# Order and queues of the first loads, and the PSUM banks of the last two value products, in windowed attention followed by a mixture of experts

## The chip, the core and the metric

The kernel runs on one core of a Trainium2 chip. A core has TensorE (PE in the profile: matmuls, with weight loads shown as PEld), VectorE (DVE), ScalarE (ACT), GpSimd (POOL) and SyncE (SP), which here only issues DMAs. ScalarE and GpSimd can issue DMAs too. The metric is the device time of one execution in microseconds (us), the median of several runs.

## What is computed

Eight batches of eight heads, 576 positions, head width 64. Attention looks back over a window of 64 positions. Its result, 4608 tokens of width 512, goes to a mixture of experts: each token goes to the one expert of eight with the largest logit, passes two weight matrices with a ReLU between them, and is scaled by the softmax weight of its expert.

```
scores = q @ k.T / 8                       # batch 8, heads 8, S = 576, D = 64
mask   = (rel >= 0) & (rel < 64)           # rel = query position - key position
attn   = softmax(where(mask, scores, -1e9))
x      = (attn @ v) as (4608, 512)
logits = x @ w_gate                        # 8 experts
e      = argmax(logits);  gate = softmax(logits)[e]
y      = gate * (relu(x @ w1[e]) @ w2[e])  # w1[e]: 512 x 1024, w2[e]: 1024 x 512
```

## The kernel before

**Tiling.** Two batches (`BG` = 2) form a group, two heads a pair; a pair in a group of batches is a *unit*. There are `NU` = 16 units, four to each group. A unit has nine tiles of 128 positions, of which three make a *step*; so `N` = 48 steps, three (`NST`) to a unit.

**Stages of a step.** They are functions, and each is written for its own step number:

- `turned(s)` (L578): PE turns q and k (L595, or L587 for the last 64 positions of the sequence, the *rests*), and ScalarE copies the result to SBUF (L600, L590).
- `scored(s)` (L606): PE multiplies q and k into banks 0 and 1, one for each head (L628).
- `masked(s)` (L634): VectorE adds the mask and takes the row's extreme (L641). `softened(s)`: ScalarE takes the exponential (L651).
- `flipped(s)` (L654): PE turns the weights (L659). VectorE copies the first head's half to SBUF, ScalarE the second's (both L661).
- `weighted(s)` (L665): PE multiplies the weights with v into a tile `px` in bank 6 (L674). v carries a column of ones, so that the row's sum comes with it.
- `divided(s)` (L680): VectorE takes the reciprocal of the sum and multiplies (L684, L685, L688), which empties `px`.
- `x_turned(s)` (L693) and `logit(s)` (L704): PE turns the result (L699, copy L702) and multiplies with the gate's weights `wg` (L711, bank 7).

**Order.** Every engine works through its instructions in program order, which is written out by hand in `step(s)` (L941): scores of step s+1, values of s-1, flip of s, division of s-1, turn of s+3, and so on. In its middle, at each unit's first step, it issues the loads ahead: `load_v(u + 2)` and `load_qk(u + 3)`, and `load_rests` once for each group. Work listed in `todo` is issued at its step, among it the load of w1 of expert 0 in four parts of 512 KB, on ScalarE's queue (L933), at steps 1, 2, 4 and 5. The loop starts at step -3, so `turned(0)` to `turned(2)` and `scored(0)` come before step 0.

**Loads.** `load_qk(u)` (L537) makes eight DMAs of 128 KB: for each batch q of both heads, then k of both heads. `load_rests(bg)` (L548) makes six DMAs for a group of batches: two each of q, k and v. `load_v(u)` (L561) makes four DMAs of 128 KB, after which GpSimd makes a copy of v that is shifted by 64 positions (L567, L569, L573). All these are issued by SyncE, in the program's order. There are slots for eight loads in flight that SyncE and ScalarE share: in the built program each load waits for the landing of the one eight places before it. q and k have three buffers, v has three.

**End of attention.** After the last step, `weighted(N - 1)` runs, then `turn()` (L302) turns the first gathered tokens of expert 0 (L306, copied by ScalarE, L307), the last logits and divisions follow, and `hidden(0)` (L336) starts the first expert's tile: its products go to banks 0, 1 and 6 (`hps`, L264). From there on it is expert after expert, tile after tile.

The lines of the first loads before the change:

```
        load_qk(0)
        nc.sync.dma_start(out=wg[:, :, 0:E], in_=moe_w_gate.rearrange("(g p) e -> p g e", p=P))
        nc.sync.dma_start(out=x_dram[NT : NT + 1, :], in_=zrow[:])
        load_rests(0)
        load_v(0)
        load_qk(1)
        load_v(1)
        load_qk(2)
```

Of the kernel before, what the change touches and what calls it, by code (L numbers as in the profile page):

```python
# [36 lines left out]
def kernel(  # L37
# [10 lines left out]
    nc = tc.nc  # L48
# [74 lines left out]
    banks = [Memory(banks_p.tile([P, 512], F32, name=f"bank{i}")) for i in range(8)]  # L123
# [110 lines left out]
    VW = D + 1  # L234
    ST = 3
# [260 lines left out]
    with tc.manual_schedule(), ExitStack() as held, ExitStack() as brief:  # L496
# [32 lines left out]
        qks, rests, Ts, xss, xTs, lgs, logits_of = {}, {}, {}, {}, {}, {}, {}  # L529
# [7 lines left out]
        def load_qk(u):  # L537
            bg, g = units[u]
            qks[u] = [qk_m(((u % 3 + 2) % 3 * 2 + n) * 1024, BG, NV, 2, D) for n in range(2)]
            for i in range(BG):  # L540
                for t, src in zip(qks[u], (q, k)):
                    for h in range(2):
                        nc.sync.dma_start(
                            out=t[:, i, :, h, :],
                            in_=src[bg * BG + i, 2 * g + h, 0:SM, :].rearrange("(p j) d -> p j d", j=NV),
                        )

        def load_rests(bg):  # L548

            at = 6144 + bg % 2 * 2048  # L550
            vr = qk_m(at + 1024, BG, H, D)
            rests[bg] = [qk_m(at, H, D), qk_m(at + 512, H, D), vr]
            for t, src in zip(rests[bg], (q, k)):
                for i in range(BG):
                    nc.sync.dma_start(
                        out=t[i * D : (i + 1) * D], in_=src[bg * BG + i, :, SM:S, :].rearrange("h p d -> p h d")
                    )
            for i in range(BG):
                nc.sync.dma_start(out=vr[D:P, i], in_=v[bg * BG + i, :, SM:S, :].rearrange("h p d -> p h d"))

        def load_v(u):  # L561
            bg, g = units[u]
            va, vb = v_ring[u % NVR]
            for i in range(BG):
                for h in range(2):
                    nc.sync.dma_start(out=va[:, i, :, h, 0:D], in_=whole(v, u, i, h))
                G.tensor_copy(out=vb[D:P, i, NV - 1, :, 0:D], in_=rests[bg][2][D:P, i, 2 * g : 2 * g + 2])  # L567

                nc.gpsimd.tensor_copy(  # L569
                    out=vb[0:D, i].rearrange("p j h d -> p (j h d)"),  # L570
                    in_=va[D:P, i].rearrange("p j h d -> p (j h d)"),
                )
                nc.gpsimd.tensor_copy(  # L573
                    out=vb[D:P, i, 0 : NV - 1].rearrange("p j h d -> p (j h d)"),
                    in_=va[0:D, i, 1:NV].rearrange("p j h d -> p (j h d)"),
                )
# [25 lines left out]
        def blocks_of(t):  # L602

            return [(t // NV, t % NV * 2 + a) if t < BG * NV else (a, NB - 1) for a in range(2)]
# [60 lines left out]
        def weighted(s, pTs):  # L665
            u, c = divmod(s, NST)
            bg, g = units[u]
            va, vb = v_ring[u % NVR]
            px = banks[6](0, 2, ST, VW)
            for m in range(ST):  # L670
                for a, (bp, i) in enumerate(blocks_of(c * ST + m)):
                    vt = va[:, bp, i // 2] if i % 2 or i == 0 else vb[:, bp, i // 2 - 1]
                    for h in range(2):
                        nc.tensor.matmul(  # L674
                            px[a * D : (a + 1) * D, h, m, :], lhsT=pTs[h][:, m, a * D : (a + 1) * D],
                            rhs=vt[:, h, :], start=True, stop=True, skip_group_check=True,
                        )
            return px
# [240 lines left out]

        N = NU * NST  # L920
        load_qk(0)
        nc.sync.dma_start(out=wg[:, :, 0:E], in_=moe_w_gate.rearrange("(g p) e -> p g e", p=P))
        nc.sync.dma_start(out=x_dram[NT : NT + 1, :], in_=zrow[:])
        load_rests(0)
        load_v(0)
        load_qk(1)
        load_v(1)
        load_qk(2)

        for g in range(NG):  # L930
            step = NST * (g // 2) + g % 2 + 1
# [9 lines left out]
        def step(s):  # L941
            if 0 <= s + 1 < N:
                prs[s + 1] = softened(*masked(s + 1, scored(s + 1)))
            if 0 <= s - 1 < N:
                px = weighted(s - 1, pTs.pop(s - 1))
# [5 lines left out]
            if s >= 0 and s % NST == 0:  # L951
                u = s // NST
                if u + 3 < NU and (u + 3) % NG == 0:
                    load_rests((u + 3) // NG)
                if u + 2 < NU:
                    load_v(u + 2)
                if u + 3 < NU:
                    load_qk(u + 3)
# [25 lines left out]
        tr_ring = cycle((4, 5))  # L984
        tile0 = chain(hidden(0), turn(), output(0))
        px = weighted(N - 1, pTs.pop(N - 1))
        form_all(turn())
        logit(N - 3)
# [170 lines left out]
```

## Time and profile before

| What | us |
|---|---|
| Median of 3 runs (718.85 to 719.68) | 719.0 |
| The profiled execution | 719.24 |
| Its span, first to last instruction | 717.5 |
| PE busy | 687.2 (96%) |
| PE weight loads busy | 606.0 (84%) |
| VectorE busy | 505.1 (70%) |
| GpSimd busy | 355.2 (50%) |
| ScalarE busy | 259.9 (36%) |

The profile shows one execution. The 1.7 us between the span and its time lie around the program. In the slices of the page each digit is a share in tenths over 17.9 us; `PEclk` is the clock that TensorE was granted. In a timeline each row is a run of like instructions: start, length, engine, line of the kernel, operation, tile written and tiles read, shape and count, and in brackets how long the engine was idle before it and what ended that. A `q` behind an engine's name means its queue, here the issue of a DMA: the row's length is the issue alone, and the data land later, by the page's medians 4.0 us after the issue for q, 3.7 for k, 4.2 for v and 4.4 for a part of w1. Attention lies in the first 217 us, the experts behind it. DMA loads of q, k and v move in packets of 256 bytes: 117072 of the 137608 packets are under 512 bytes.

### The profile page before, as it was taken

The numbers are of one execution on the slowest core, as the hardware profiler recorded it, in microseconds if no ns is written. First come the engines' busy times: TensorE is split into PE (matmuls) and PEld (weight loads), VectorE is DVE, ScalarE is ACT, GpSimd is POOL, SyncE is SP. The second block draws the span as 40 slices with busy tenths as digits, with TensorE's granted clock in tenths as the row PEclk, the third lists the DMA queues.
The fourth block names the chain that finished last, engine by engine and source line by source line (L and its number), as shares of the span: only waits on it lengthen the run. The fifth ranks groups of instructions, "written<-read, shape, count | busy, mean of one in ns | idle before, by whom it ended". The sixth has DMA issues, their size and how long they took to land. (4 is left out here: it accounts for less than half of the span.)

```text
span 717.5 us, 17980 instructions
## 1 busy us (share of the span) xinstructions
PE 687.2 (96%) x6882; PEld 606.0 (84%) x6882; DVE 505.1 (70%) x1656; ACT 259.9 (36%) x655; POOL 355.2 (50%) x366
## 2 busy tenths in 40 slices
PE   4999999999879999999999999999999999999995
PEld 3787888788668898797999999899979799979995
DVE  3576898798965858685866676586667586666764
ACT  4688888788754211111211221121111121112210
POOL 4213847669376025947562257356274756263012
PEclk9899999999999999999999999999999999999999
DMA  8998889989261382716211441450171531111021
GB/s 156 219 198 182 179 167 226 223 187 244 87 193 48 124 294 67 275 61 195 104 46 61 148 144 61 123 200 34 60 274 60 189 109 46 60 38 45 16 61 57
DMA packets 137608, 94.42 MB, mean 132 GB/s; under 512 B 117072, under 2 KB 117072, under 8 KB 137490
## 3 DMA queue, kind: packets, MB, share of 16 engines
q1 hardware_dynamic: 127858, 62.16, 32.6%
q0 software_dynamic: 9056, 28.58, 12.5%
q10 hardware_dynamic: 576, 2.10, 0.9%
q8 instruction: 74, 1.21, 0.7%
q14 instruction: 44, 0.36, 0.2%
HBM read 73.94 MB, written 20.45 MB: 132 GB/s over the span
## 5 line engine op out<-in xcount | busy, mean ns | idle before, releaser
L315 DVE STREAM_TRANSPOSE v_m<-qk_m 32x256 f32<-32x256 f32 x320 | 139.3, 435 | 8.6 <-DMA qk_m<-x_dram,at_g 2.7
L275 POOL DMA_INDIRECT qk_m<-x_dram,at_g x42 | 45.4, 1081 | 176.1 <-DVE v_m L315 147.1
L344 PE MATMUL bank<-qk_m,s 128*128 128x128 f32 x1024 | 122.5, 275 | 0.6 <-DVE qk_m L365 0.6
L344 PEld LDWEIGHTS bank<-qk_m,s 128*128 128x128 f32 x1024 | 118.3, 192 | 0.8 <-issue 0.8
L651 ACT ACTIVATE pr<-pr,mx 128x128 f32<-128x128 f32 x288 | 89.7, 390 | 33.1 <-DVE mx L641 32.9
L344 PE MATMUL bank<-qk_m,w 128*128 128x128 f32 x768 | 93.8, 275 | 0.8 <-DVE v_m L384 0.8
L344 PEld LDWEIGHTS bank<-qk_m,w 128*128 128x128 f32 x768 | 90.6, 192 | 4.3 <-issue 4.0
L641 DVE CUSTOM_DVE_ANT_0 pr<-bank,mask 128x128 f32<-128x128 f32 x288 | 64.4, 286 | 28.3 <-PE bank L628 26.8
L384 DVE TENSOR_TENSOR v_m<-bank,v_m 128x256 f32<-128x256 f32 (+1 forms) x95 | 43.8, 480 | 40.8 <-PE bank L388 25.9
L295 POOL DMA_INDIRECT out_dram<-v_m,at_s x42 | 42.5, 1013 | 54.1 <-DVE v_m L384 50.4
L569 POOL COPY v_m<-v_m 64x520 f32<-64x520 f32 x32 | 19.8, 619 | 69.9 <-DMA v_m<-in_v_dram 69.1
L140 POOL TENSOR_TENSOR s<-w 128x1024 f32<-128x1024 f32 x22 | 52.2, 2375 | 0.0
L674 PEld LDWEIGHTS bank<-v_m,pT 128*64 128x64 f32 x1152 | 40.9, 140 | 12.5 <-DVE xs L688 6.7
L674 PE MATMUL bank<-v_m,pT 128*64 128x65 f32 x1152 | 47.7, 231 | 3.6 <-DVE xs L688 3.6
L351 ACT COPY qk_m<-bank 128x512 f32<-128x512 f32 x16 | 9.4, 587 | 108.6 <-PE bank L344 70.3
L388 PE MATMUL bank<-qkT_m,v_m 128*128 128x256 f32 x216 | 48.3, 379 | 0.0
L595 PE MATMUL bank<-ident,qk_m 128*128 128x128 f32 x256 | 36.8, 287 | 9.4 <-DMA qk_m<-in_q_dram 8.4
L388 PEld LDWEIGHTS bank<-qkT_m,v_m 128*128 128x128 f32 x216 | 41.0, 190 | 5.5
L327 ACT COPY qk_m<-v_m 128x512 f32<-128x512 f32 x40 | 22.7, 615 | 62.4 <-DVE v_m L315 62.4
L444 PEld LDWEIGHTS bank<-qk_m,w 128*128 128x128 f32 x320 | 43.9, 190 | 0.9 <-issue 0.7
L444 PE MATMUL bank<-qk_m,w 128*128 128x160 f32 x320 | 44.4, 299 | 0.4 <-ACT qk_m L327 0.4
L628 PE MATMUL bank<-qkT_m 64*64 64x128 f32 x1152 | 44.2, 284 | 0.1
(174 smaller groups left out, 1252.6 us busy)
## 6 DMA issues: line engine op xcount, KB each, us to landing
w<-in_moe_w_dram SPq DMA_DIRECT2D x11, 2048.0 KB, 9.7
qk_m<-in_q_dram SPq DMA_DIRECT2D x72, 128.0 KB, 4.0
qk_m<-in_k_dram SPq DMA_DIRECT2D x72, 128.0 KB, 3.7
v_m<-in_v_dram SPq DMA_DIRECT2D x64, 128.0 KB, 4.2
qk_m<-in_moe_w_dram SPq DMA_DIRECT2D x3, 2048.0 KB, 11.2
x_dram<-xs POOLq DMA_DIRECT2D x6, 512.0 KB, 4.8
x_dram<-xs POOLq DMA_DIRECT2D x3, 768.0 KB, 5.2
w<-in_moe_w_dram ACTq DMA_DIRECT2D x4, 512.0 KB, 4.4
```

Of the source, the lines that this page charges most:

```text
L140: op()
L275: G.indirect_dma_start(out=xg[c], out_offset=None, in_=x_dram[:, :], in_offset=bass.IndirectOffsetOnAxis(ap=at_g[:, c : c + 1], axis=0),)
L295: put = G.indirect_dma_start(out=out[:, :], out_offset=bass.IndirectOffsetOnAxis(ap=at_s[:, c : c + 1], axis=0), in_=ys[c], in_offset=None ...
L315: V.transpose(out=xn[b * QD : (b + 1) * QD, :, :, a * QD : (a + 1) * QD].rearrange("p c g i -> p (c g) i"), in_=rows[a * QD : (a + 1) * QD ...
L344: nc.tensor.matmul(acc[:, f, :], lhsT=a[:, g, f * P : (f + 1) * P], rhs=b[:, g, :], start=(first and f == 0 and g == 0), stop=(g == HG - 1 ...
L384: plus = lambda out, a, b: V.tensor_tensor(out=out, in0=a, in1=b, op=ALU.add)
L388: nc.tensor.matmul(acc, lhsT=a[:, f, :], rhs=b[:, f, :], start=(start and f == 0), stop=(stop and f == HF - 1), skip_group_check=True,)
L444: nc.tensor.matmul(acc[:, i], lhsT=w1[:, g, f * P : (f + 1) * P], rhs=xq[:, g].rearrange("p c s -> p (c s)")[:, 0:HALF], start=(i + g == 0 ...
L628: nc.tensor.matmul(out_, lhsT=qT[rows, t, a * WINDOW : (a + 1) * WINDOW], rhs=rhs, start=True, stop=True, skip_group_check=True,)
L641: V.tensor_tensor_reduce(out=prs[h][:, m, :], in0=scs[h][:, m, :], in1=mask[:, m0 + m, :], scale=-scale, scalar=-2 * MASKED, op0=ALU.add, ...
L651: nc.scalar.activation(out=y, in_=y, func=AF.Exp, scale=-1.0, bias=mx[:, h, m : m + 1])
L674: nc.tensor.matmul(px[a * D : (a + 1) * D, h, m, :], lhsT=pTs[h][:, m, a * D : (a + 1) * D], rhs=vt[:, h, :], start=True, stop=True, skip_ ...
```

## The change

Three things are edited. The k loads of unit 0 and of group 0's rests (six DMAs) are issued by ScalarE instead of SyncE. The order of the first loads is new: the rests and unit 1's q and k come before v, `wg` stands behind v of unit 1, and the zero row behind unit 2's q and k. And `weighted` of the last two steps, N-2 and N-1, puts its result in banks 0 and 1 instead of bank 6; `divided` reads it there.

```diff
@@ load_qk
-                for t, src in zip(qks[u], (q, k)):
+                for t, src, queue in zip(qks[u], (q, k), (nc.sync, nc.sync if u else nc.scalar)):
                     for h in range(2):
-                        nc.sync.dma_start(
+                        queue.dma_start(
@@ load_rests
-            for t, src in zip(rests[bg], (q, k)):
+            for t, src, queue in zip(rests[bg], (q, k), (nc.sync, nc.sync if bg else nc.scalar)):
                 for i in range(BG):
-                    nc.sync.dma_start(
+                    queue.dma_start(
@@ weighted
-            px = banks[6](0, 2, ST, VW)
+            px = banks[6 if s < N - 2 else s - N + 2](0, 2, ST, VW)
@@ the first loads
         load_qk(0)
+        load_rests(0)
+        load_qk(1)
+        load_v(0)
+        load_v(1)
         nc.sync.dma_start(out=wg[:, :, 0:E], in_=moe_w_gate.rearrange("(g p) e -> p g e", p=P))
+        load_qk(2)
         nc.sync.dma_start(out=x_dram[NT : NT + 1, :], in_=zrow[:])
-        load_rests(0)
-        load_v(0)
-        load_qk(1)
-        load_v(1)
-        load_qk(2)
```

On ScalarE the six DMAs stand ahead of everything else in its program, the load of its function table (1.28 us, issued with the first L600) included. In the new order of slots, unit 2's last k load is the one that waits for the landing of w1's first part, and unit 3's first q load the one that waits for its second part.

## The prediction

> **What bounds the kernel now.** I read the page first (busy time by slice), then who TensorE waited for, then the timeline of single engines where those waits lie.
>
> From the page, part 2:
>
> ```profile
> PE   4999999999879999999999999999999999999995
> ...
> PEclk9899999999999999999999999999999999999999
> DMA  8998889989261382716211441450171531111021
> ```
>
> TensorE (PE) is over 90% busy in all but four slices of 17.9 us. Three of the four can matter here: the first, where loads arrive, and slices 11 and 12 (179 to 215 us), where attention ends. Elsewhere the span is PE's own work, so an earlier start of it moves the end one for one.
>
> All waits of PE in the whole run (microseconds in total, times, longest):
>
> ```profile
> PE bank L595 <- DMA qk_m<-in_q_dram: 8.4, 4, 4.8
> PE bank L674 <- DVE xs L688: 3.6, 6, 1.2
> ...
> PE bank L587 <- DMA qk_m<-in_k_dram: 1.3, 1, 1.3
> PE bank L595 <- DMA qk_m<-in_k_dram: 0.8, 3, 0.4
> ```
>
> Line 1 is the turning of q and k (`turned`), line 2 the values' product (`weighted`) waiting until VectorE has emptied bank 6 (`divided`). These two are what the change touches. SyncE's queue at the start:
>
> ```profile
> 6.31 0.55 SPq L922 DMA_DIRECT2D wg<-in_moe_w_gate_dram  x1
> ...
> 11.46 2.53 SPq L566 DMA_DIRECT2D v_m<-in_v_dram  x4
> 14.03 1.24 SPq L543 DMA_DIRECT2D qk_m<-in_q_dram  x2
> 15.32 1.30 SPq L543 DMA_DIRECT2D qk_m<-in_k_dram  x2
> 16.67 1.30 SPq L543 DMA_DIRECT2D qk_m<-in_q_dram  x2
> 18.01 1.30 SPq L543 DMA_DIRECT2D qk_m<-in_k_dram  x2
> ```
>
> One load of 128 KB takes 0.67 us of the queue, and unit 1's q starts only at 14.03. What PE makes of it:
>
> ```profile
> 13.42 0.30 PE L587 MATMUL bank<-ident,qk_m 128*128 128x128 f32 x1 [1.28 <-DMA qk_m<-in_k_dram]
> ...
> 18.48 2.29 PE L595 MATMUL bank<-ident,qk_m 128*128 128x128 f32 x8 [2.62 <-DMA qk_m<-in_q_dram]
> 20.70 1.56 PE L628 MATMUL bank<-qkT_m 64*64 64x128 f32 x24
> 22.19 1.62 PE L674 MATMUL bank<-v_m,pT 128*64 128x65 f32 x24
> ```
>
> A wait for loads comes back once, at unit 4 (same view, later window):
>
> ```profile
> 55.99 0.63 PE L595 MATMUL bank<-ident,qk_m 128*128 128x128 f32 x4 [0.64 <-DMA qk_m<-in_q_dram]
> 57.02 0.63 PE L595 MATMUL bank<-ident,qk_m 128*128 128x128 f32 x4 [0.41 <-DMA qk_m<-in_k_dram]
> ```
>
> So between 24 and 57 us PE is full, yet the load stream is no more than just ahead of it. By stretch (the last two figures are the DMA engines' busy share and GB/s):
>
> ```profile
> 15.00:23.00 8.00, 5.27 (x51) 3.87 (x51) 1.99 (x16) 3.56 (x10) 2.83 (x6) 0.50 1.06 214
> ```
>
> With one queue issuing, the DMA engines already show a share of 1.06 at 214 GB/s, which is 0.61 us for 128 KB, close to the queue's 0.67. The end of attention, PE:
>
> ```profile
> 213.48 0.97 PE L674 MATMUL bank<-v_m,pT 128*64 128x65 f32 x24 [0.48 <-DVE xs L688]
> ...
> 216.81 0.97 PE L674 MATMUL bank<-v_m,pT 128*64 128x65 f32 x24 [0.88 <-DVE xs L688]
> 217.71 1.09 PE L306 MATMUL bank<-ident,qk_m 128*128 128x128 f32 x8
> ```
>
> **What the Trainium skill says.** "DMA: Bandwidth & Descriptors", section on issuing engines not being separate DMA queues: loads from several engines run on the same 16 DMA engines, and a second issuer saves only issue time. The 1.06 above agrees: there is little rate left to win. "Perfetto Trace Analysis", section on the HWDGE DMA instruction: an issue's reported time includes a wait for an exclusive descriptor generator. Whether ScalarE's and SyncE's issues take turns there, no row of this trace shows. "TensorE: Matmul & The Clock Gate", Part 1: the clock is halved after a window of 3.4 us with little work, in windows not tied to the kernel's start. The trace agrees: 15 to 23 us ran at 0.50. "ScalarE: Activation LUTs", section on the cost of the table load: about 1283 ns; the trace has 1.28 us.
>
> **The change part by part.** The profiled execution took 719.24 us (span 717.5), 0.24 above the median of 719.0; the sum is made against 719.24.
>
> (a) Six k loads leave SyncE's queue: 6 x 0.67 = 4.0 us less for it ahead of everything later. That is the upper end of what the stream can win if issue alone binds. If the DMA engines bind, the first 26 loads (8 of unit 0, 6 rests, 8 of unit 1, 4 of v of unit 0) take 26 x 0.61 = 15.9 us; from about 2.4 us, when the first bytes move, plus 0.6 to report, the last lands near 18.9. Before, the last of them was issued at 18.7, and a k load took 3.7 us from issue to landing (the page's median), so near 22.4: 3.5 won. I take 3.5 and keep 3.0 to 4.0.
>
> (b) wg, the zero row, v of units 0 and 1 move behind unit 1's q and k. In sum they stay in the stream ahead of unit 4, so the stream wins nothing by it, but PE's early waits change. Unit 1's q and k are issued from about 7.5 instead of 14.03, so the 2.62 us wait at 18.48 goes, and so does the 1.28 us at 13.42. What is late next: v of unit 0. It moves behind, lands near 18, and GpSimd then copies for 0.62 + 0.51 us (L569, L573), so `weighted` of step 0 runs at about 18.5 instead of 22.19. That is 3.7 earlier, plus up to 1 us if PE's clock rises sooner. v of unit 1 also lands before q and k of unit 2 now; unit 2 is needed by PE from 32 us on, less the shift, and lands by 29. wg is needed at 31.0 (L711) and lands before 21. The zero row is needed only by gathers at the end.
>
> (c) ScalarE issues six loads before its table load: 4 x 0.65 at once, then two that wait for a slot. In the program's order every load waits for the landing of the load eight places earlier, over both queues; for these two it is the landing of the first two k loads. Queued behind them are the table load and the first copies of `turned`, for which `scored` waits. ScalarE is free at about 5.8, the table load ends near 7.1 and the first copy starts there instead of 5.90. PE needs the first pair of copies only after its 16 turns, at about 5.2 + 16 x 0.27 = 9.6, and they end by 8.4: hidden, with 1.2 us to spare. If issues take turns at 1.3 us each, the first copy slips to about 9, and step 0 loses about 1 us; that is hidden under the wait for v of unit 0 in (b).
>
> (d) Loads meet w1's four loads of 512 KB, which ScalarE issues at steps 1, 2, 4 and 5. They come earlier with the steps. A SyncE load whose slot is held by one of them waits for it: before, the four v loads at 28.07 took 5.10 us instead of 2.5. Now the load that waits is unit 2's last k. Bound: from 1 us better to 1.5 worse; I take 0.
>
> From (a) to (d): PE would be 4 us or more ahead after step 1, but at unit 4 it waits for the stream again and keeps the stream's 3.5 us.
>
> (e) The banks. `weighted` of the last two steps writes banks 0 and 1, last read by `masked` of the last step, done near 210.5. So the waits of 0.48 and 0.88 us for L688 go. What is late next is ScalarE's copy of the turned weights (L661): for the first it ends at 213.15 (212.67 + 0.48), so 0.33 of 0.48 is won. For the second it ends at 216.16 (215.68 + 0.48), 0.33 earlier by the shift, so 215.83 against 216.81: 0.98 in all. After it comes `turn` (L306), which needs the gather issued at 212.85 with 3.5 us to land, 216.35; it would start at 216.73. Product x of the first tile uses bank 0 and y bank 1, both emptied by `divided` before PE gets there. Won: 0.9, bounds 0.3 and 1.0.
>
> Sum: 3.5 + 0.9 = 4.4 us. 719.24 - 4.4 = 714.8; on the median's footing 714.6.
>
> **The rivals.**
> A. The stream isn't what holds PE. With fewer collisions it stays ahead, unit 4's wait (0.64 + 0.41) goes, and PE keeps all that it wins at the start: the distance from step 2's `scored` at 25.96 to about 20.5 if its clock rises at once, 5.5. In all 5.5 + 1.05 + 0.9 = 7.45: 711.6. For it: the wait at unit 4 is only 1 us. Against it: the DMA share of 1.06.
> B. The engines are full from the first loads, two queues only interleave, and the win at the start is gone at unit 4. The banks' 0.9 and a few tenths stay: 717.9. For it: the DMA row's 8 and 9. Against it: the first slice, with wg and the zero row in it, has room.
> C. Slower: the shared slots. Unit 2's last k waits for the first w1 load, which ScalarE issues only in step 1, and SyncE's whole queue stands behind it. Before, the same kind of wait cost 2.6 us (5.10 less 2.5 at 28.07). It takes all that the stream won when it stands 2.6 + 3.5 = 6.1 us; at 8 us unit 4 is 2 us later than before: 719.24 + 2 - 0.9, 720.1 on the median's footing. For it: the queue's order fixes that wait. Against it: the w1 load takes 4.4 us from issue to landing (page), so 8 us needs a late issue as well.
>
> **How the numbers follow.** Main 0.70, A 0.13, B 0.09, C 0.08. About 0.2% (1.4 us) is what a measurement of this kernel can tell from no change. Main and A are faster: 0.83; B lies within: 0.09; C is slower: 0.08. The range runs from A's 711.6 to 717.0, where the stream wins 1.3 us only; B and C, 0.17, are left out.
>
> **What would show it.** Right: no wait of PE for q between 12 and 20 us, `weighted` of step 0 near 18.5, a wait at unit 4 of 1 us or more, and no wait for L688 in the last two steps. Wrong: no wait at unit 4 (A), `scored` of step 12 no earlier than before (B), SyncE standing over 6 us near 24 us (C).

## The result, and the profile after

| | before | after |
|---|---|---|
| Median of the comparison, 11 runs each (us) | 719.14 | 716.25 |
| Ratio | | 0.9966 [0.995, 0.9983] |
| The profiled execution (us) | 719.24 | 715.43 |
| Its span (us) | 717.5 | 713.7 |

The ratio is worth 2.4 us of 719 (1.2 to 3.6). The forecast was 4.4 us. The sign was right and the time lies in the range, but the gain was sized too large.

Part 2 of the page after, in slices of 17.8 us:

```profile
PE   6999999999889999999999999999999999999995
PEclk9999999999989999999999999999999999999999
DMA  9997889979443273616201531440271521111011
```

The first slice has filled from 4 to 6. Slice 12, at the end of attention, went from 7 to 8. The waits of PE in the whole run after (us in total, times, longest):

```profile
PE bank L595 <- DMA qk_m<-in_q_dram: 1.2, 2, 0.6
...
PE bank L674 <- POOL v_m L573: 0.8, 1, 0.8
...
PE bank L674 <- DVE xs L688: 0.7, 2, 0.5
PE bank L595 <- DMA qk_m<-in_k_dram: 0.6, 2, 0.4
```

Waiting for q fell from 8.4 to 1.2, but 4.8 of this is only a label: PE's very first wait, for the first load in before, is now put down to the mask, and it has grown to 5.8 us. Without the first wait the fall is 8.4 - 4.8 - 1.2 = 2.4 us. Waiting for L688 fell from 3.6 to 0.7. PE's timeline after, around step 0's values and at unit 4:

```profile
16.15 1.91 PE L595 MATMUL bank<-ident,qk_m 128*128 128x128 f32 x8
17.99 0.89 PE L628 MATMUL bank<-qkT_m 64*64 64x128 f32 x24
18.81 0.62 PE L674 MATMUL bank<-v_m,pT 128*64 128x65 f32 x8
20.23 0.74 PE L674 MATMUL bank<-v_m,pT 128*64 128x65 f32 x16 [0.80 <-POOL v_m L573]
20.90 0.87 PE L659 MATMUL bank<-ident,pr 128*128 128x128 f32 x6
...
53.30 0.63 PE L595 MATMUL bank<-ident,qk_m 128*128 128x128 f32 x4 [0.65 <-DMA qk_m<-in_q_dram]
54.37 0.63 PE L595 MATMUL bank<-ident,qk_m 128*128 128x128 f32 x4 [0.44 <-DMA qk_m<-in_k_dram]
```

No wait for q is left near 16 us. `weighted` of step 0 starts at 18.81 and stops once for GpSimd's copy (0.80). The wait at unit 4 is still there, 0.65 + 0.44 us, 2.7 us earlier than in before. The end of attention, PE after:

```profile
205.67 1.62 PE L674 MATMUL bank<-v_m,pT 128*64 128x65 f32 x24
...
209.54 1.29 PE L674 MATMUL bank<-v_m,pT 128*64 128x65 f32 x24
...
212.30 1.21 PE L674 MATMUL bank<-v_m,pT 128*64 128x65 f32 x24
213.44 1.09 PE L306 MATMUL bank<-ident,qk_m 128*128 128x128 f32 x8
```

The last two rows of L674 carry no wait for L688 any more. Their lengths, 1.29 and 1.21 us instead of 0.97, hold a pause for ScalarE's copy of the second head's weights (in the later one it ends at 212.54, and PE goes on at 212.59). From the start of `weighted` of step N-3 to `turn` (L306) it is 7.77 us, against 8.68 in before (209.03 to 217.71).

In this pair of profiles the lead over before (start of the last L628 matmul of a step) is 3.23 us at step 2, 2.65 at step 11, the first after unit 4's turn, 1.2 to 1.4 at steps 24 to 29, 4.15 at step 45, and 3.8 at the end. This pair of profiles therefore shows more than the ratio does, and the lead is not constant. The experiments had to say which part of this the change makes. Steps are counted here as in `scored(s)`. The recorded texts count the rows a little differently: the scores at 25.96 us in before, their step 2, are step 3 here, and those at 57.9 us, their step 12, are step 11.

### The profile page after: what moved, and what is told of

It reads as the page before. It is cut to its first block, busy times and chain, and to the rows that moved or that the text cites. A ratio compares the mean times of both kernels' runs of the same rounds, so it can differ in the third digit from the quotient of the medians.

```text
span 713.7 us, 17981 instructions
## 1 busy us (share of the span) xinstructions
PE 688.6 (96%) x6882; PEld 606.9 (85%) x6882; DVE 505.0 (71%) x1656; ACT 260.3 (36%) x655; POOL 355.9 (50%) x366
## 3 DMA queue, kind: packets, MB, share of 16 engines
q8 instruction: 74, 1.21, 0.7%
## 5 line engine op out<-in xcount | busy, mean ns | idle before, releaser
L569 POOL COPY v_m<-v_m 64x520 f32<-64x520 f32 x32 | 19.8, 620 | 70.6 <-DMA v_m<-in_v_dram 69.7
L674 PEld LDWEIGHTS bank<-v_m,pT 128*64 128x64 f32 x1152 | 41.0, 139 | 10.7 <-issue 4.8
L674 PE MATMUL bank<-v_m,pT 128*64 128x65 f32 x1152 | 48.1, 229 | 1.6 <-POOL v_m L573 0.8
L628 PE MATMUL bank<-qkT_m 64*64 64x128 f32 x1152 | 45.6, 287 | 0.5 <-DVE mx L641 0.3
L595 PE MATMUL bank<-ident,qk_m 128*128 128x128 f32 x256 | 36.3, 287 | 7.7 <-POOL mask L517 5.8
```

The costliest lines, as they stand in the source:

```text
L628: nc.tensor.matmul(out_, lhsT=qT[rows, t, a * WINDOW : (a + 1) * WINDOW], rhs=rhs, start=True, stop=True, skip_group_check=True,)
L674: nc.tensor.matmul(px[a * D : (a + 1) * D, h, m, :], lhsT=pTs[h][:, m, a * D : (a + 1) * D], rhs=vt[:, h, :], start=True, stop=True, skip_ ...
```

## The experiments

The theory was the prediction's: the loads win about 3.5 us, limited at unit 4 by the stream of loads, and the banks 0.9. Its rivals were that the stream wins hardly anything, and that what is won is lost later. Four kernels took the change apart.

**e1, the banks alone.** The loads are those of before.

```diff
-            px = banks[6](0, 2, ST, VW)
+            px = banks[6 if s < N - 2 else s - N + 2](0, 2, ST, VW)
```

> The banks alone; loads and queues as before. Theory: the waits for L688 in the last two steps go and nothing else moves, so the distance from weighted of step N-3 to the first turn (L306), 8.7 us before, falls by 0.9 to 1.0; scored of step 12 starts where it did (57.9 us, within 0.3); time 718.2. Rival (the copies of the turned weights or the first tile take the wait over): the distance falls by under 0.4 and the time by under 0.4.

Measured: 716.25 us beside 717.45, ratio 0.998 [0.9965, 0.9994], 1.4 us (0.4 to 2.5). The end of attention took 7.93 us, a gain of 0.75. The banks work without the loads. But this profile was already 1.0 us ahead of before at step 11, where both kernels have done the same and 0.3 was allowed: executions differ by that much.

**e2, the loads alone:** the changed kernel with bank 6 to the end.

```diff
-            px = banks[6 if s < N - 2 else s - N + 2](0, 2, ST, VW)
+            px = banks[6](0, 2, ST, VW)
```

> The loads and their queue alone; the values stay in bank 6. Theory: scored of step 12 starts 2.6 us earlier, as in the changed kernel, the distance of the tail stays 8.7, and the time is 0.9 us above that of the changed kernel, about 717. Rival (the two parts need each other): scored of step 12 earlier by less than 2.

Measured: 715.98, ratio 0.9972 [0.9959, 0.9986], 2.0 us (1.0 to 2.9), where the prediction had 3.5. Its lead was 4.66 us at step 2, 0.24 at step 3 and 1.00 at step 11, where 2.6 was expected; under 2 was the sign of its rival. Between steps 2 and 3 PE waited 1.27 us for v and 0.80 for its copy, and then ran at half clock.

**e3, the order alone,** all loads on SyncE (from e2):

```diff
-zip(qks[u], (q, k), (nc.sync, nc.sync if u else nc.scalar))
+zip(qks[u], (q, k), (nc.sync, nc.sync))
...
-zip(rests[bg], (q, k), (nc.sync, nc.sync if bg else nc.scalar))
+zip(rests[bg], (q, k), (nc.sync, nc.sync))
```

> The new order alone: all loads on SyncE, bank 6. Theory (the stream of loads as a whole sets the lead at unit 4): scored of step 2 starts about 2 us earlier, but at step 12 the lead is at most 0.5 us, and the time is that of before within 0.5. Rival (the early waits of PE are what counts, unit 4's wait is chance): the lead of step 2 is still there at step 12, 2 us or more, and the time is about 717.

**e4, the second queue alone,** the first loads in the order of before (from e2):

```diff
         load_qk(0)
-        load_rests(0)
-        load_qk(1)
-        load_v(0)
-        load_v(1)
         nc.sync.dma_start(out=wg[:, :, 0:E], in_=moe_w_gate.rearrange("(g p) e -> p g e", p=P))
-        load_qk(2)
         nc.sync.dma_start(out=x_dram[NT : NT + 1, :], in_=zrow[:])
+        load_rests(0)
+        load_v(0)
+        load_qk(1)
+        load_v(1)
+        load_qk(2)
```

> The six k loads on ScalarE alone: old order, bank 6. Theory (stream): scored of step 12 starts 2.2 to 3.0 us earlier, all that the changed kernel has there; time about 717. Rival (order counts): lead at step 12 under 1.5 us.

Measured: e3 718.01, ratio 1.001 [0.9993, 1.0027]; e4 715.87, ratio 0.9975 [0.9963, 0.9986], 1.8 us. The leads at step 11 were 0.63 (at most 0.5 expected) and 1.64 us (2.2 to 3.0 expected, under 1.5 for the rival). The new order wins nothing that can be measured when it stands alone; the second queue wins in the old order as much as in the new one. The landings say how little that is in the stream itself. The 30th load of 128 KB (unit 1's last v) landed at 25.27 us in before, at 23.85 in e3 and at 22.98 in the changed kernel. The step from before to e3 comes with `wg` and the zero row, which only moved behind it. So the second queue is worth 0.9 us here, and 0.4 in e2 (23.49). In the timed runs e2 and e4 are both about 2 us faster than e3. Where the rest of that comes from is not shown.

The next three ask what holds PE at unit 4, where the loads of w1 run in between.

**e5, w1 later.** The changed kernel; w1 is loaded nine steps later, and its sums on GpSimd follow seven steps later.

```diff
-            step = NST * (g // 2) + g % 2 + 1
+            step = NST * (g // 2) + g % 2 + 10
...
-            todo.setdefault(3 * NST + n, []).append(op)
+            todo.setdefault(16 + n, []).append(op)
```

> The changed kernel with w1's four parts loaded at steps 10, 11, 13 and 14 and its sums formed from step 16 on, so that 2 MB leave the stream ahead of unit 4. Theory (the stream of loads is what PE waits for at unit 4): both waits there go (1.1 us), and scored of step 12 starts 3.5 to 4.5 us earlier than in the unchanged kernel, against 2.65; time 1 to 2 us under the changed kernel's. Rival (PE's own early steps set the lead): lead at step 12 under 3, time the same.

Measured: 719.2 beside 717.81, ratio 1.0034 [1.0017, 1.0052]. At the start it does what the theory says. The issue of unit 2's last two k loads, in SyncE's queue after:

```profile
25.02 3.46 SPq L543 DMA_DIRECT2D qk_m<-in_k_dram  x2
```

and the same row in e5:

```profile
25.58 1.30 SPq L543 DMA_DIRECT2D qk_m<-in_k_dram  x2
```

Two loads need 1.30 us; the other 2.16 is the wait for the slot that w1's first part holds. Without it, and with w1's 2 MB out of the stream, unit 4's second k landed at 50.83 instead of 54.23, PE's wait at unit 4 was gone, and the lead at step 11 was 4.09 us, as expected. The time was not: later more than this was lost, and e5 is 1.4 us slower than before. PE in e5:

```profile
76.18 0.42 PE L711 MATMUL bank<-xT,wg 128*32 128x128 f32 x6 [1.30 <-ACT lgT L722]
...
109.91 0.55 PE L699 MATMUL bank<-ident,xs 128*128 128x128 f32 x3 [1.66 <-DVE pT L661]
```

w1's sums, 2.4 us each on GpSimd, now lie at 95 to 108 us, among its copies of v and its weighing of x (L813). That these collide is read from the rows' places and does not cover the wait at 76.18; no run separates it from the later load.

**e6, q and k ahead of v.** In `step`, `load_qk(u + 3)` moves ahead of `load_rests` and `load_v(u + 2)`.

```diff
+                if u + 3 < NU:
+                    load_qk(u + 3)
                 if u + 3 < NU and (u + 3) % NG == 0:
                     load_rests((u + 3) // NG)
                 if u + 2 < NU:
                     load_v(u + 2)
-                if u + 3 < NU:
-                    load_qk(u + 3)
```

> The changed kernel with load_qk(u + 3) issued ahead of the rests and of v of unit u + 2 in each unit's first step. In all the same loads; unit 4's q and k move ahead of ten others. Theory: the waits at unit 4 go, lead at step 12 of 3.5 to 4.5 us, unless v of unit 2 or 3 is late instead, which would show as weighted waiting for GpSimd's copies; time 1 to 2 us under the changed kernel's. Rival: the lead at step 12 stays under 3.

**e7, both edits together.**

> Both of these edits. Theory: no more than the better of the two, lead at step 12 about 4.4, because the waits at unit 4 are gone with either. Rival: they add up to over 5.

Measured: e6 718.71, ratio 1.0011 [0.9998, 1.0024]; e7 724.12, ratio 1.0088 [1.0065, 1.0112]. In e6 unit 4's second k landed at 46.95 and no wait for q or k was left there. Now v of unit 3 was late (PE waited 0.80 us for L573 at 57.82), and the lead fell from 3.71 us at step 11, which is what was expected there, to 1.14 at step 12 and below zero by step 20. In e7 the lead at step 11 was 1.33, and `weighted` once waited 4.29 us for L688, because VectorE waited 4.56 us for a store of x (`DMA x_dram<-xs`) before it could write the next tile. In these three kernels taking the wait at unit 4 away wins nothing in the time: something else is late further on.

**e8, the rests' k back on SyncE.** The changed kernel, with four k loads on ScalarE instead of six, and all four issued before any slot is full.

```diff
-zip(rests[bg], (q, k), (nc.sync, nc.sync if bg else nc.scalar))
+zip(rests[bg], (q, k), (nc.sync, nc.sync))
```

> The changed kernel with the rests' k back on SyncE, so that ScalarE issues four loads and none that waits for a slot: its table load ends near 4.8 instead of 7.1. Theory (the table load is hidden, and two loads more on SyncE cost the stream 1.3 us): scored of step 0 within 0.3 us of the changed kernel's, lead at step 12 of 1.3 to 2.2 us against 2.65. Rival (ScalarE's late start costs): scored of step 0 at least 0.5 us earlier and the lead at step 12 over 2.65.

Measured: 714.49 beside 717.81, ratio 0.9953 [0.9937, 0.9969], the best of all. The price of two loads more on SyncE, 2 x 0.67 = 1.3 us lost, did not appear: the lead at step 11 was 2.85. Nor does ScalarE's late start cost: the table load ended at 4.81 us, and the scores of step 0 still started 0.7 us later than in the changed kernel (10.91 against 10.19). Whether e8 really beats the changed kernel was asked again on another chip, where before had a median of 718.14.

**r_before, r_after, r_rests_sp:** before, the changed kernel and e8 once more. **e9:** e8 with bank 6 to the end.

> The kernel before once more, unchanged, as the yardstick for ratios of 0.2 to 0.5%. Theory: its ratio to before is 1 within 0.15%. In its profile, against the first profile of before, the start of scored at steps 2, 11 and 29 may lie up to 1 us to either side, since the kernel with only the banks changed showed 0.8 us there with the same first loads; a rival is that such shifts are caused by the edits, and then this profile repeats the first within 0.3 us.

> The changed kernel once more, unchanged. Theory: ratio 0.9966 within 0.15%; the lead over before is 2 to 4 us at step 2, about 2.5 us at unit 4, where PE again waits for q and k for about 1 us in all; in the middle of attention it falls by 1 us or more; the end of attention is 0.8 us shorter than before's 8.68 us.

> The changed kernel with the two k loads of the rests back on SyncE, once more. Theory: the DMA engines set the pace of the first loads, so that two loads more or less on the second queue change nothing: ratio to before 0.9965, like the changed kernel's, and the first result of 0.9953 was the scatter of the comparison. Rival: with ScalarE's queue free of the two loads that waited for a slot, something is really won: 0.995 again, 1 us less than the changed kernel beside it.

> The same with bank 6 for the last two steps: only four k loads on ScalarE and the new order. Theory: 0.0013 to 0.0020 (the banks' 0.9 us, and the 0.2% that the banks alone measured) above the kernel with the banks beside it, so 0.9978 if that one is at 0.9965; the end of attention 8.7 to 8.8 us, with waits for L688 again. Rival, that the banks' gain is hidden by what follows (gathers, the first expert's tile): the same ratio within 0.0005.

| Kernel | Median (us) | Ratio to before |
|---|---|---|
| r_before | 718.07 | 0.9999 [0.9978, 1.002] |
| r_after | 716.37 | 0.9965 [0.995, 0.998] |
| r_rests_sp | 716.01 | 0.9963 [0.9948, 0.9979] |
| e9, four k, bank 6 | 717.04 | 0.9978 [0.9959, 0.9998] |

The changed kernel repeats its ratio. e8's 0.9953 does not come again: it is not shown to be better than the changed kernel, and two loads more or less on ScalarE's queue make no difference that can be seen. The banks are worth 0.0015 here (e9 against r_rests_sp, 1.1 us, with overlapping intervals).

The repeated profile of the changed kernel was the surprise. Its lead over before was 4.85 us at step 2, 0.01 at step 3, and 0.02 at step 11. PE in this second execution of the same kernel:

```profile
18.82 0.45 PE L674 MATMUL bank<-v_m,pT 128*64 128x65 f32 x2 [1.55 <-DVE mx L641]
20.84 0.70 PE L674 MATMUL bank<-v_m,pT 128*64 128x65 f32 x6 [1.58 <-DMA v_m<-in_v_dram]
22.09 1.19 PE L674 MATMUL bank<-v_m,pT 128*64 128x65 f32 x16 [0.55 <-POOL v_m L573]
23.21 1.54 PE L659 MATMUL bank<-ident,pr 128*128 128x128 f32 x6
```

Compare the rows from 18.81 on in the first execution. The second load of v landed at 20.71 instead of 18.85, so the last sixteen matmuls of `weighted` start 1.86 us later. And the clock, which had been full from 11.8 us on, is at half from 18.6 to 25.4 us: `flipped` (L659) takes 1.54 us instead of 0.87. In the first execution it was at half until 17.9 us (eight of L595 took 1.91 us at 16.15 and 1.04 at 21.61) and then full. Late v and half clock turn 1.62 us ahead of the first execution at step 2 into 3.37 behind at step 3 (26.57 against 23.20). What follows is carried on by the slots; unit 2's k in SyncE's queue of this execution:

```profile
25.58 5.75 SPq L543 DMA_DIRECT2D qk_m<-in_k_dram  x2
```

It stood 5.75 us, since ScalarE issued w1's first part only at 26.07 instead of 22.69, as its program order has it behind step 1. So the stream is late as well, and unit 4's k with it. The profiled executions in us, without e7, whose second k of unit 4 has no record:

| Execution | Step 3's scores | w1's first part issued | Unit 4's second k landed | Step 11's scores | Span |
|---|---|---|---|---|---|
| before / r_before | 26.58 / 26.36 | 26.08 / 25.85 | 56.88 / 56.31 | 58.52 / 57.94 | 717.5 / 716.0 |
| e1 | 25.61 | 25.11 | 55.87 | 57.51 | 714.7 |
| r_after | 26.57 | 26.07 | 56.87 | 58.51 | 713.9 |
| e2 | 26.34 | 25.76 | 55.89 | 57.52 | 714.2 |
| e9 | 26.86 | 25.83 | 56.50 | 58.14 | 714.1 |
| e3 | 26.69 | 26.18 | 56.26 | 57.89 | 715.5 |
| after | 23.20 | 22.69 | 54.23 | 55.87 | 713.7 |
| e8 / r_rests_sp | 23.50 / 23.30 | 23.00 / 22.80 | 54.03 / 53.65 | 55.67 / 55.28 | 712.5 / 712.0 |
| e4 | 23.11 | 22.61 | 55.24 | 56.88 | 715.4 |
| e6 | 23.82 | 23.32 | 46.95 | 54.81 | 716.7 |
| e5 | 23.91 | 58.00 | 50.83 | 54.44 | 717.0 |

Except in e5 and e6, step 11 follows unit 4's k by 1.6 us in every row, so the stream does set PE's time there. And where step 3 is late, the stream is too. With the new order and k loads on both queues, step 3 came before 24 us in five profiled executions (after, e5, e6, e8, r_rests_sp) and after 26 us in four (r_after, e2, e9, and e7 with 26.66). Where the landing of unit 0's second v is on record, it parts the kernels with the new order in the same way: 18.85 to 19.47 us where step 3 is early, 20.03 to 20.75 where it is late (r_after, e2, e9 and e3).

It would be easy to say that this mixture makes 1.5 us in the timed runs out of the 2.65 in the shown profile. The spans don't bear it out: r_after is 2.64 us behind after at step 11 and 0.24 at the end, and it still ends 2.0 us ahead of r_before. A part of this lies at the end of attention, where PE waits for VectorE in every profile:

```profile
202.67 1.58 PE L914 MATMUL bank<-hi_e,lo 128*128 128x4 bf16 x54 [2.70 <-DVE hi_e L907]
```

During this wait, or within 2.5 us of its end, the clock falls to half, for 6.8 us in eight of the fourteen profiles (r_before and after among them) and for 3.4 us in six (before and r_after among them). An estimate from these figures: 3.4 us more at half clock cost PE up to 1.7 us, as much as the gain in question. How the early and the late executions are shared among the timed runs isn't known; their times show no two groups.

The end of attention, by kernels. With the new banks: 7.77 (after), 7.71 (r_after), 7.93 (e1), 7.83 (e8), 7.23 (r_rests_sp), 7.83 (e5 and e6), 7.30 (e7), mean 7.68. With bank 6: 8.68, 8.83 (before, r_before), 8.74 (e2), 8.80 (e3), 8.81 (e4), 8.33 (e9), mean 8.70. The difference is 1.0 us. The shortest of each kind (7.23, 7.30, 8.33) are among those with half clock for 3.4 us only. In e9 the waits are back:

```profile
210.80 0.97 PE L674 MATMUL bank<-v_m,pT 128*64 128x65 f32 x24 [1.05 <-DVE xs L688]
214.13 0.97 PE L674 MATMUL bank<-v_m,pT 128*64 128x65 f32 x24 [0.88 <-DVE xs L688]
215.03 1.09 PE L306 MATMUL bank<-ident,qk_m 128*128 128x128 f32 x8
```

## Why the prediction was right, and where it was off

**(e) The banks: right.** Predicted 0.9; measured 1.0 over fourteen profiles, and 1.4, 1.1 and 0.4 us in three pairs of timed kernels (e1 against before, r_rests_sp against e9, after against e2), of which only the first is clear of noise. The next limit is ScalarE's copy L661, as forecast: it shows as the pause inside the rows of 1.29 and 1.21 us.

**(a) The stream: the mis-sized term.** The step took 3.5 us as the difference of two landings of the 26th load, 22.4 before and 18.9 after, and said that PE keeps it at unit 4. In before this landing (unit 1's last k) is at 21.97. After, it is unit 0's last v, which has a record only in e5 and e7 among the kernels with the changed kernel's first loads: 20.84 and 21.86. So 0.1 to 1.1 us are won there. The pace of 0.61 us for a load explains a part. From 15 to 19 us it was right (222 GB/s after), but earlier it was slower, and from 2.4 to 19 us the changed kernel moved 206 GB/s and e5 200 (0.64 and 0.66 us for a load), which makes 0.7 to 1.2 us in 26 loads. The rest lies between the moving of the bytes and the landing, for which the step took 0.6 us; why it is longer isn't shown. The last three figures of these rows are clock, share and GB/s, first of before, then after:

```profile
5.00:10.00 5.00, 4.17 (x20) 2.73 (x23) 0.00 (x0) 1.77 (x4) 2.56 (x7) 1.00 0.71 152
5.00:10.00 5.00, 3.62 (x16) 3.14 (x16) 0.00 (x0) 3.01 (x4) 2.59 (x7) 1.00 1.37 197
```

"DMA: Bandwidth & Descriptors", section on issuing engines not being separate DMA queues, says that transfers started by different engines interleave on the same 16 DMA engines, and that a second issuer saves only the time to issue. The traces agree: where one queue already moved 215 GB/s (15 to 19 us), two moved 222. But where it left room, as in the row of 152 GB/s, the saved issue time did raise the rate. The share is no measure of this room: from 10 to 15 us it rose from 1.06 to 1.37, and the rate only from 186 to 190. Measured in time, the loads win 2.0 (e2), 1.6 (e9) and 1.0 us (after against e1). Rival B, "a few tenths", was too low, and rival A, 5.5 us, too high; but in r_after the lead at step 11 was 0.02, which the prediction had named as the sign of B.

**(b) The early waits: right up to step 3 in five of nine profiles.** The waits for q went, and `weighted` of step 0 started at 18.81, forecast 18.5. The step named v of unit 0 as what is late next. It did not price v landing later than the second scores, which costs 1.3 to 1.8 us of waiting in r_after, e2 and e9, 3.2 in e7, and then half clock. Before, v was ahead of unit 1's q and k and landed by 17.21; e3 and e4 together say that moving it behind them wins nothing that can be measured.

**(c) ScalarE: right.** The first copy was at 7.12, forecast 7.1. The queues and ScalarE after:

```profile
0.79 2.99 SPq L543 DMA_DIRECT2D qk_m<-in_q_dram  x4
0.81 2.71 ACTq L543 DMA_DIRECT2D qk_m<-in_k_dram  x4
7.12 1.26 ACT L600 COPY qkT_m<-bank 128x512 f32<-128x512 f32 x2
```

Four issues on ScalarE took 2.71 us and four on SyncE beside them 2.99, so they do not take turns at 1.3 us each. PE's first turn started 1.0 us later than in before (5.82 against 4.78), with q and k sharing the DMA engines. The step left that out.

**(d) The slots: 0 taken, bounds -1 to +1.5.** In the shown profile it fits: unit 2's last k waited 2.16 us, the last four v of before about as long (5.10 less 2.5), and the lead at unit 4 was 2.65. In r_after the wait was 4.45 us, and the lead 0.02. So rival C's mechanism is real: it passes a lateness of step 1 on. Whether it also costs something where step 1 is early isn't shown, since e5 took this wait and w1's 2 MB away together. The lead differs by 2.6 us between two executions of one kernel, which is a little more than the bounds had room for.

**The path between unit 4 and the end: not in the prediction.** "Elsewhere the span is PE's own work, so an earlier start of it moves the end one for one" is where the sum was too simple. At step 30 of before:

```profile
129.38 0.56 DVE L688 TENSOR_TENSOR xs<-bank,rec 128x384 f32<-128x384 f32 x1 [2.01 <-DMA x_dram<-xs]
```

VectorE waited for a store of x, and PE then 1.15 us for VectorE. The same wait stands in e8 (1.98 us) and not in after or r_before. The two profiles of before differ by 1.5 us in span, as much as the gain in question. This is a part of why the shown pair has 3.8 us and the ratio 2.4: against r_before the span after is 2.3 us shorter.

## What to carry to other kernels

- A second queue for the first loads saves issue time, and that helps only where one queue leaves the DMA engines room. Before pricing it, read the GB/s in each stretch, and compare landings, not issues, of the same load.
- When a load moves behind others, ask what it feeds and whether it then lands later than its reader's other inputs: the cover may hold in one execution and not in the next, and shared slots hand a late step on to the loads behind it.
- Where one gain is 0.3% of the time, profile the same kernel twice before explaining a difference between two traces, and compare how long the clock was at half in each.

## What the runs showed of the hardware

- TensorE's clock is a lottery at the start. In two executions of the changed kernel it was at half until 17.9 us and then full in one, and full from 11.8 and at half from 18.6 to 25.4 in the other, where PE had waited for v. "TensorE: Matmul & The Clock Gate", Part 1, has windows of 3.4 us that are not tied to the kernel's start; the 6.8 us are two of them. Nor is it a lottery at the start alone: at the end of attention the same wait of 2.7 us (L914) goes with one window at half in six profiles and with two in eight, and in e7 the clock fell to half at 131.4 us, for 6.8 us, near the end of a wait of 4.29 us. That the waits decide it, and not the phase alone, is argued, not shown.
- VectorE's small bf16 comparison (L802, 128x128) took 0.30 us alone and 0.66 beside GpSimd's copy L569 at 99.67, which kept its 0.62 us. "SBUF — State Buffer", section on the two separate sides, has the two engines share a pair of ports as an exclusive lock. Here the row ends 0.06 us after the copy (100.35 against 100.29), which is sooner than 0.30 us of work after a full block would; spans on GpSimd are rough, and no run here separates the lock from another cause.
- Why one load of v landed 5.0 us after its issue in r_after (15.73 to 20.71) and 3.7 in after (15.18 to 18.85) stays open. One thing goes with it. In each of the fourteen profiles exactly one of SyncE's issues between 17.9 and 21.7 us takes 1.5 to 2.1 us instead of about 0.6, and a DMA of 16 KB of the kind that the page calls `instruction` starts within 0.3 us of it. Among the kernels with the new order it is v's sixth load or an earlier one where step 3 is late (in r_after at 17.93), and the eighth or something behind it where step 3 is early (in after at 18.59). No run moves this stop alone, so it is a lead and not a cause.
